# Filler matmuls in the waits of a kernel's boot, with one score buffer fewer (RWKV-6 attention and a dense pair, fp32)

## The chip, the core and the metric

The kernel runs on one core of one Trainium2 chip. The metric is the device time of one execution in microseconds (us). A core has a matrix engine (TensorE, PE in the profile, its weight loads PEld), a vector engine (VectorE, DVE), a scalar engine (ScalarE, ACT), GpSimd (POOL) and SyncE (SP), which here only issues transfers. [...]

## The reference, cut to what matters

```python
# attention: r, k, v, w of (4, 8, 768, 48), u of (8, 48)
for t in range(S):
    cur = np.einsum('bhd,bhe->bhde', u[None] * kt, vt)
    y[:, :, t] = np.einsum('bhd,bhde->bhe', rt, state + cur)
    state = wt[:, :, :, None] * state + np.einsum('bhd,bhe->bhde', kt, vt)
# x: y as (3072, 384); w_in (384, 2048), w_out (2048, 384)
h = x @ w_in
g = h - np.tanh(h)
return g @ w_out
```

Each head carries a 48x48 state through 768 time steps, with a decay w per step. The result, with the heads beside each other, goes through two dense layers. All of it is fp32.

## The kernel before, in words

The work is cut into eight blocks: four batches by two halves of the sequence (384 steps each). A block has an attention part and a dense part. The dense part of block i runs while the attention part of block i+1 is laid between its matmuls, by a plan written out by hand (`plan`, L531). For the first block there is no dense part to hide behind: its attention is done by `boot` (L565) at the start of the kernel. The order of instructions on TensorE, VectorE, ScalarE and SyncE is that of the program.

The attention of a block works on 64-step chunks. Heads lie in pairs, two heads of 48 in one tile of 128 partitions; the four pairs form two halves, h1 (pairs 2 and 3) and h2 (pairs 0 and 1). The scores of a chunk are built by levels. Level 1 takes products of neighbouring steps, with u, from the tiles `rmix` and `kmix` (made by ScalarE and VectorE in `mix`, L220 and L222). Levels 2, 4, 8, 16 and 32 multiply blocks of ever greater size. For each, `gram` (L242) does 24 small matmuls per half from `kq` and `rp`; `decay` (L274, VectorE) then multiplies `kq` and `rp` in place by the decays, so it must wait until TensorE has read them, and the next level of that half must wait for the decay; VectorE writes the scores from PSUM under a mask (L249 and L302), or at level 16 ScalarE copies them (L295). `totals` (L260) multiplies the decays of neighbouring blocks. At level 32 (`last_level`, L319) the copies by ScalarE (L330) are put off until after `turn`.

Then `turn` transposes `kq` on TensorE (L342) and ScalarE copies it to `ks` (L344); `update` multiplies it by v (L360), and VectorE carries the state over the chunks, twelve dependent steps for each half (L371). The result of a half is the sum of two sets of 24 matmuls in one pair of PSUM tiles: scores by v (`from_scores`, L406) and states by r (`from_states`, L388); between the sets TensorE drains and waits for it (`fence`, L418 and L424). In the boot, h1 takes the scores first and then the states, h2 the states first. ScalarE copies the result to `late` and `xT` (L434), a few small transfers fill holes in `xT`, and the first dense matmul (L484) can begin. A later block's inputs and the dense weights are loaded during the boot too; some of these transfers begin behind a given instruction (`begin_behind`).

All PSUM tiles of the attention come from `scratch` (L178): a tile of two banks in a pool. In the boot the pool has four such tiles[...]. A tile can be used again when what reads it is done. After the boot the pool is replaced by others.

The dense part takes 16 slices of 128 hidden columns: three matmuls for h (L484), an activation made of ScalarE and VectorE operations (L491 to L509), and three matmuls for the output (L522) three slices later.

Of the kernel before, what the change touches and what calls it, by code (L numbers as in the profile page):

```python
# [37 lines left out]
F32 = mybir.dt.float32  # L38
# [6 lines left out]
PSUM = bass.MemoryType.PSUM  # L45
# [3 lines left out]
P = 128  # L49
L = 64  # L50
NB = 384
# [33 lines left out]
def kernel(  # L85
# [10 lines left out]
    nc = tc.nc  # L96

    const = ctx.enter_context(tc.tile_pool(name="const", bufs=1))
# [13 lines left out]
    u_sb = const.tile([P, NPAIR], F32, name="u_sb", tag="u_sb")  # L112
    nc.scalar.dma_start(out=u_sb, in_=uT)

    warm = const.tile([P, 1], F32, name="warm", tag="warm")
    nc.scalar.activation(out=warm, in_=shift[:, 0:1], func=AF.Copy)

# [47 lines left out]
    def convert(f, raw, _):  # L165

        lo, hi = raw[:, :, 0], raw[:, :, 1]
        a = w_sb[:, f, :].bitcast(I32)
        up = conv.tile([P, 2 * DM], I32, name="up", tag="up", bufs=3)
        nc.scalar.activation(out=a.bitcast(F32), in_=hi.bitcast(F32), func=AF.Prelu,  # L170
                             scale=HIGH_SCALE, alpha=NEGATIVE)
        nc.scalar.activation(out=up, in_=lo.bitcast(U32), func=AF.Copy, scale=2.0 ** -29)
        return [
            lambda: nc.vector.tensor_single_scalar(a, a, 3, op=ALU.logical_shift_left),
            lambda: nc.vector.tensor_tensor(out=a, in0=a, in1=up, op=ALU.add)]  # L175
# [372 lines left out]
    blocks = [Block(b, q) for b in range(B) for q in range(NQ)]  # L548
# [3 lines left out]
    def more_weights(queue):  # L552
        raws.append(load_weights(more_weights.n, queue))
        more_weights.n += 1
        return raws[-1][-1]
# [3 lines left out]
    def begin_behind(ins, dma):  # L559


        tc.add_manual_dep(dma.ins, ins.ins.name, mybir.DependencyInfo(
            mybir.DependencyClass.Sync, mybir.DependencyReason.DATA))

    def boot(ps, blk, later):  # L565

        h1, h2 = HALVES
        for p0 in HALVES:
            for name, src in (("kq", kT), ("rp", rT), ("wt", wT)):
                blk.load(name, src, p0, UP)  # L570
        for name in ("rmix", "kmix"):
            blk.tiles[name] = inp.tile([P, NPAIR * NB], F32, name=name, tag=name)
        more_weights(nc.sync)
        blk.load_v()
        for _ in range(2):
            more_weights(nc.sync)
        blk.mix(h1, UP, copy=nc.vector.tensor_copy)
        masked = blk.level_1(ps, h1)
        blk.decay(1, h1, UP)
        blk.totals(1, h1, UP)  # L580
        blk.mix(h2, UP, copy=nc.scalar.copy)
        masked()
        blk.level(ps, 2, h1, UP)
        masked = blk.level_1(ps, h2)
        blk.decay(1, h2, UP)
        blk.totals(1, h2, UP)
        for m in (2, 4, 8, 16):
            blk.totals(m, h1, UP)
        masked()
        background = {2: lambda: later.load("rmix", rT, 0, NPAIR), 8: lambda: later.load("kmix", kT, 0, NPAIR),  # L590
                      16: lambda: later.load("wt", wT, 0, NPAIR), 32: lambda: more_weights(nc.sync)}
        ready, last = [], []
        for m in (2, 4, 8, 16, 32):
            for p0 in HALVES:
                if (m, p0) != (2, h1):
                    ins = blk.level(ps, m, p0, UP, last)
                if p0 == h2 or m == 32:
                    blk.totals(m, p0, UP)
            if m in background:
                begin_behind(ins, background[m]())  # L600
            if m <= 8:
                ready.append(convert(*raws.pop(0)))
            if m == 8:
                later.mix(0, NPAIR, ("rmix",))

        def converted():
            for op in ready.pop(0):
                op()

        more_weights(nc.sync)  # L610
        for p0 in HALVES:
            blk.turn(ps, p0)
        for copies in last:
            copies()
        later.mix(0, NPAIR, ("kmix",))
        for p0 in HALVES:
            blk.update(ps, p0)

        blk.result_2(*blk.result_1(ps, [h1, h1 + 1], "from_scores"), True, "from_states")
        blk.fill_holes([nc.sync, nc.scalar, nc.gpsimd])  # L620
        converted()
        ready.append(convert(*raws.pop(0)))
        converted()
        ins = blk.result_2(*blk.result_1(ps, [h2, h2 + 1]), True)
        begin_behind(ins, more_weights(nc.sync))
        later.load("kq", kT, 0, NPAIR)
        later.load("rp", rT, 0, NPAIR)
        while ready:
            converted()
        for name in ("totals 1", "totals 2"):  # L630
            later.prepare(name)
        for name in ("kq", "rp"):
            ready.append(convert(*raws.pop(0)))
            converted()
            later.prepare(name)

    with tc.tile_pool(name="ps_boot", bufs=4, space=PSUM) as ps_boot:
        xT = blocks[0].begin()
        boot(ps_boot, blocks[0], blocks[1])
    ps_d = ctx.enter_context(tc.tile_pool(name="ps_d", bufs=1, space=PSUM))  # L640
    ps_a = ctx.enter_context(tc.tile_pool(name="ps_a", bufs=2, space=PSUM))
    waiting, rest, extra = [], [], []
# [11 lines left out]
    for i, blk in enumerate(blocks):  # L654
        here = xT
        later = blocks[i + 1] if i + 1 < len(blocks) else None
# [5 lines left out]
        for f in range(NF):  # L662
# [15 lines left out]
            name, ins = loads.get(f), None  # L678
# [67 lines left out]
```

## Time and profile before

| | us |
|---|---|
| median of 4 runs (666.69 to 668.73) | 667.31 |
| profiled execution | 665.43 |
| its span, first to last instruction | 663.3 |
| TensorE busy | 641.4 |
| VectorE busy | 545.1 |
| ScalarE busy | 489.8 |
| first dense matmul (L484) starts at | 42.73 |
| first output matmul (L522) starts at | 56.99 |

All times inside a profile count from the start of the span. One fp32 matmul of the program stands in the profile as two MATMUL records and two LDWEIGHTS records; a transpose as one of each. "Idle before" is the time in which the engine stood before an instruction, with what ended it; "issue" means that the profile shows nothing that it waited for. PEclk is the share of TensorE's clock that was granted. The q8 queue of the transfers carries instructions.

### The profile page before, as it was taken

The numbers are of one execution on the slowest core, as the hardware profiler recorded it, in microseconds if no ns is written. First come the engines' busy times: TensorE is split into PE (matmuls) and PEld (weight loads), VectorE is DVE, ScalarE is ACT, GpSimd is POOL, SyncE is SP. The second block draws the span as 40 slices with busy tenths as digits, with TensorE's granted clock in tenths as the row PEclk, the third lists the DMA queues.
The fourth block names the chain that finished last, engine by engine and source line by source line (L and its number), as shares of the span: only waits on it lengthen the run. The fifth ranks groups of instructions, "written<-read, shape, count | busy, mean of one in ns | idle before, by whom it ended". The sixth has DMA issues, their size and how long they took to land.

```text
span 663.3 us, 19968 instructions
## 1 busy us (share of the span) xinstructions
PE 641.4 (97%) x8480; PEld 408.8 (62%) x8480; DVE 545.1 (82%) x1101; ACT 489.8 (74%) x968; POOL 4.8 (1%) x19
## 2 busy tenths in 40 slices
PE   5869999999999999999999999999999999999997
PEld 4745556566665666666666666656666566665554
DVE  7789999899768997599886997689975899757764
ACT  4779999876768667785767758686677857778785
POOL 2000000000000000000000000000000000000000
PEclk9969999999999999999999999999999999999999
DMA  8756433431303122221212231123131200000001
GB/s 319 232 180 224 132 130 121 142 121 50 97 11 115 54 67 80 58 72 53 94 50 57 74 97 52 50 64 112 49 97 29 101 3 2 1 12 37 0 0 37
DMA packets 30841, 54.37 MB, mean 82 GB/s; under 512 B 2336, under 2 KB 28704, under 8 KB 30752
## 3 DMA queue, kind: packets, MB, share of 16 engines
q1 hardware_dynamic: 30336, 52.80, 24.8%
q8 instruction: 67, 1.10, 0.7%
q10 hardware_dynamic: 352, 0.25, 0.1%
q14 instruction: 22, 0.18, 0.1%
q0 software_dynamic: 64, 0.05, 0.0%
HBM read 47.19 MB, written 4.72 MB: 78 GB/s over the span
## 4 chain that ended last, share of the span: by engine, by line
PE 86%; DVE 7%; ACT 2%; DMA 2%; issue 2%; PEld 0%; SPq 0%; PEldq 0%; DVEq 0%
PE acc L522 36%; PE hp L484 34%; PE att L242 8%; PE att L406 2%; PE att L388 2%; PE att L342 2%; PE att L360 1%; DVE hs L501 1%; DVE rp L274 1%; PE att L319 1%; DMA kq<-in_kT 1%; DVE kq L274 1%; DVE scores L302 1%; DVE w_sb L175 1%; DMA wt<-in_wT 1%
## 5 line engine op out<-in xcount | busy, mean ns | idle before, releaser
L484 PE MATMUL hp<-xT,w_sb 128*128 128x384 f32 x768 | 272.3, 491 | 4.1 <-ACT xT L434 2.1
L522 PE MATMUL acc<-w_sb,gT 128*128 128x384 f32 x768 | 273.7, 493 | 0.8
L484 PEld LDWEIGHTS hp<-xT,w_sb 128*128 128x128 f32 x768 | 145.2, 191 | 107.2 <-ACT xT L434 2.3
L522 PEld LDWEIGHTS acc<-w_sb,gT 128*128 128x128 f32 x768 | 140.5, 190 | 89.9 <-ACT o L527 2.3
L491 ACT ACTIVATE h<-hp 128x384 f32<-128x384 f32 x128 | 62.6, 489 | 125.5 <-PE hp L484 124.7
L506 DVE TENSOR_TENSOR th<-h,th 128x384 f32<-128x384 f32 x128 | 71.1, 555 | 45.7 <-ACT th L495 45.7
L501 DVE SCALAR_TENSOR_TENSOR hs<-h,s 128x384 f32<-128x384 f32 x128 | 71.1, 556 | 25.0 <-ACT s L492 25.0
L509 DVE COPY_PREDICATED gT<-big,th 128x384 f32<-128x384 int32 x128 | 76.3, 596 | 12.4
L493 ACT ACTIVATE qa<-s,shift 128x384 f32<-128x384 f32 x128 | 78.8, 615 | 4.2
L501 DVE SCALAR_TENSOR_TENSOR gT<-qb,hs 128x384 f32<-128x384 f32 x128 | 71.4, 558 | 9.3
L496 ACT ACTIVATE big<-s,shift 128x384 f32<-128x384 f32 x128 | 76.8, 600 | 0.0
L494 ACT ACTIVATE qb<-s,shift 128x384 f32<-128x384 f32 x128 | 76.7, 600 | 0.0
L501 DVE SCALAR_TENSOR_TENSOR hs<-qa,hs 128x384 f32<-128x384 f32 x128 | 70.7, 552 | 0.0
L492 ACT ACTIVATE s<-h 128x384 f32<-128x384 f32 x128 | 67.0, 524 | 4.0
L495 ACT ACTIVATE th<-h 128x384 f32<-128x384 f32 x128 | 64.9, 507 | 0.0
L242 PEld LDWEIGHTS att<-rp,kq 48*64 48x64 f32 x3072 | 53.3, 145 | 18.1 <-issue 11.7
L242 PE MATMUL att<-rp,kq 48*64 48x32 f32 x3072 | 57.2, 229 | 1.9 <-DVE rp L274 1.1
L274 DVE TENSOR_TENSOR kq<-kq,tot 128x768 f32<-128x768 f32 (+1 forms) x45 | 38.7, 860 | 2.3 <-PE att L319 1.4
L274 DVE TENSOR_TENSOR rp<-rp,tot 128x768 f32<-128x768 f32 (+1 forms) x45 | 38.9, 865 | 0.0
L371 DVE SCALAR_TENSOR_TENSOR states<-states,tot,att 128x48 f32<-128x48 f32 x176 | 31.5, 260 | 8.9 <-PE att L360 8.9
L302 DVE COPY_PREDICATED scores<-mask_all,att 128x384 f32<-128x384 uint8 (+1 forms) x54 | 31.9, 658 | 0.0
L242 PE MATMUL att<-rmix,kmix 48*64 48x64 f32 x768 | 14.6, 233 | 7.2 <-ACT rmix L222 7.2
(54 smaller groups left out, 335.6 us busy)
## 6 DMA issues: line engine op xcount, KB each, us to landing
raw<-in_weights SPq DMA_DIRECT2D x16, 768.0 KB, 4.4
rmix<-in_rT SPq DMA_DIRECT2D x7, 768.0 KB, 4.8
kmix<-in_kT SPq DMA_DIRECT2D x7, 768.0 KB, 4.6
wt<-in_wT SPq DMA_DIRECT2D x7, 768.0 KB, 4.6
kq<-in_kT SPq DMA_DIRECT2D x7, 768.0 KB, 5.6
rp<-in_rT SPq DMA_DIRECT2D x7, 768.0 KB, 4.6
v_sb<-in_v SPq DMA_DIRECT2D x8, 576.0 KB, 4.0
out_y<-o SPq DMA_DIRECT2D x23, 192.0 KB, 1.9
```

Source lines behind the costliest of these rows:

```text
L242: nc.tensor.matmul(dst, lhsT=lhs[rows, t0:t0 + L], rhs=src, start=True, stop=True)
L274: ins = nc.vector.tensor_tensor(out=part, in0=part, in1=by, op=ALU.mult)
L484: nc.tensor.matmul(hp, lhsT=w_in_sb[:, f, kc, :], rhs=xT[:, kc, :], start=(kc == KC - 1), stop=(kc == 0))
L492: nc.scalar.activation(out=s, in_=h, func=AF.Square)
L493: nc.scalar.activation(out=qa, in_=s, func=AF.Square, bias=shift[:, 0:1])
L494: nc.scalar.activation(out=qb, in_=s, func=AF.Square, bias=shift[:, 1:2])
L495: nc.scalar.activation(out=th, in_=h, func=AF.Tanh)
L496: nc.scalar.activation(out=big, in_=s, func=AF.Relu, bias=shift[:, 2:3])
L501: return lambda: nc.vector.scalar_tensor_tensor(out=out, in0=in0, scalar=scalar, in1=in1, op0=op0, op1=ALU.mult)
L506: lambda: nc.vector.tensor_tensor(out=th, in0=h, in1=th, op=ALU.subtract),
L509: lambda: nc.vector.copy_predicated(out=g, mask=big.bitcast(I32), data=th)], made
L522: nc.tensor.matmul(acc, lhsT=g[:, j * P:(j + 1) * P], rhs=w_out_sb[:, f, :], start=(f == 0), stop=(f == NF - 1))
```

## The change

A constant tile of ones is written by VectorE at the start. A new pool holds one PSUM tile `spare` of one bank, and the boot's pool for scores has three tiles and not four. In the boot, `keep_busy(n)` does n matmuls of 128x128 by 128x384 in fp32 from the constant tile into `spare`, which nobody reads: four ahead of everything, and one after each group of score matmuls (level 1 and level 2 of h1, level 1 of h2, and then each level of each half): sixteen in all. Nothing else is changed. In the changed kernel the lines after L114 stand two to fifteen lines further down (L242 is L244, L319 is L321, L342 is L344, L360 is L362, L388 is L390, L406 is L408, L484 is L486); the filler is L575.

```diff
+    idle_in = const.tile([P, NB], F32, name="idle_in", tag="idle_in")
+    nc.vector.memset(idle_in, 1.0)
...
-    def boot(ps, blk, later):
+    def boot(ps, ps_idle, blk, later):
 
         h1, h2 = HALVES
+        spare = ps_idle.tile([P, NB], F32, name="spare", tag="spare")
+
+        def keep_busy(n):
+
+            for _ in range(n):
+                nc.tensor.matmul(spare, lhsT=idle_in[:, 0:P], rhs=idle_in, start=True, stop=True)
+
+        keep_busy(4)
...
         masked = blk.level_1(ps, h1)
+        keep_busy(1)
         blk.decay(1, h1, UP)
...
         blk.level(ps, 2, h1, UP)
+        keep_busy(1)
         masked = blk.level_1(ps, h2)
+        keep_busy(1)
         blk.decay(1, h2, UP)
...
                 if (m, p0) != (2, h1):
                     ins = blk.level(ps, m, p0, UP, last)
+                    keep_busy(1)
...
-    with tc.tile_pool(name="ps_boot", bufs=4, space=PSUM) as ps_boot:
+    with tc.tile_pool(name="ps_boot", bufs=3, space=PSUM) as ps_boot, \
+            tc.tile_pool(name="ps_idle", bufs=1, space=PSUM) as ps_idle:
         xT = blocks[0].begin()
-        boot(ps_boot, blocks[0], blocks[1])
+        boot(ps_boot, ps_idle, blocks[0], blocks[1])
```

## The prediction

> **What bounds the kernel now.** I read the page, then busy time by stretch, then groups by shape, then the time line of TensorE in the boot (0 to 42.7 us, when the first dense matmul starts). The page:
>
> ```profile
> PE 641.4 (97%) x8480; PEld 408.8 (62%) x8480; DVE 545.1 (82%) x1101; ACT 489.8 (74%) x968; POOL 4.8 (1%) x19
> PEclk9969999999999999999999999999999999999999
> ```
>
> TensorE is the bound, except in the boot, and nothing after it has slack: what the boot gains or loses reaches the end. Stretches of 5 us show the only recorded loss of clock (PEclk is the third figure from the end):
>
> ```profile
> 35.00:40.00 5.00, 3.72 (x131) 3.25 (x135) 4.57 (x7) 3.40 (x6) 1.30 (x2) 0.69 0.13 34
> 40.00:45.00 5.00, 2.93 (x32) 1.81 (x24) 4.44 (x9) 3.80 (x7) 0.00 (x0) 0.50 0.54 173
> ```
>
> The half clock lasts from 36.85 to 47.09 us. Before 30 us the record says full, but the durations don't: the same shapes, first in the boot, then later.
>
> ```profile
> L242 PE MATMUL att<-rp,kq 48*64 48x32 f32 x379 | 12.0, 292 | 1.6 <-DVE rp L274 1.1 <-issue 0.4
> ...
> L342 PE MATMUL att<-ident,kq 128*128 128x128 f32 x12 | 2.8, 422 | 0.0
> ...
> L242 PE MATMUL att<-rp,kq 48*64 48x32 f32 x2304 | 38.4, 220 | 0.0
> ...
> L342 PE MATMUL att<-ident,kq 128*128 128x128 f32 x72 | 8.8, 273 | 0.0
> ```
>
> So TensorE is cold up to 30 us (in L360 the step between matmuls falls there from 27 to 15 ns). The time line (start, length, what, count, idle before and its releaser):
>
> ```profile
> 6.29 1.56 PE L242 MATMUL att<-rmix,kmix 48*64 48x64 f32 x48 [6.29 <-ACT rmix L222]
> 7.97 1.51 PE L242 MATMUL att<-rp,kq 48*64 48x32 f32 x48
> 10.36 1.56 PE L242 MATMUL att<-rmix,kmix 48*64 48x64 f32 x48 [0.89 <-ACT rmix L222]
> 12.45 2.35 PE L242 MATMUL att<-rp,kq 48*64 48x32 f32 x78 [0.53 <-DVE rp L274]
> 15.24 2.13 PE L242 MATMUL att<-rp,kq 48*64 48x32 f32 x66 [0.44 <-issue]
> 17.90 6.03 PE L242 MATMUL att<-rp,kq 48*64 48x32 f32 x187 [0.53 <-DVE rp L274]
> 24.09 0.43 PE L242 MATMUL att<-rp,kq 48*64 48x32 f32 x5 [0.16 <-issue]
> 24.45 0.76 PE L319 MATMUL att<-rp,kq 48*32 48x32 f32 x48
> 25.74 0.74 PE L319 MATMUL att<-rp,kq 48*32 48x32 f32 x48 [0.54 <-DVE tot L260]
> 26.41 2.82 PE L342 MATMUL att<-ident,kq 128*128 128x128 f32 x12
> 29.16 1.99 PE L360 MATMUL att<-v_sb,ks 64*64 64x48 f32 x96
> 31.29 0.55 PE L406 MATMUL att<-scores,v_sb 64*48 64x64 f32 x24
> 32.58 0.54 PE L406 MATMUL att<-scores,v_sb 64*48 64x64 f32 x21 [0.74 <-ACT scores L330]
> 35.10 0.31 PE L406 MATMUL att<-scores,v_sb 64*48 64x64 f32 x3 [1.98 <-issue]
> 35.50 0.99 PE L388 MATMUL att<-rp,states 48*48 48x64 f32 x52
> ```
>
> Two readings. From 9.6 to 24 us VectorE is never idle (4.90 and 5.00 of 5 us at 10 and at 15): its 1.45 to 1.6 us per half of a level pace the levels, and it waits for TensorE once, 0.66 us at 24.56. And TensorE stops three times in the middle of a group, for nothing but "issue": after 222 matmuls, 253 more (66+187) and 254 more (5+48+48+12+96+24+21). With a load each and some semaphore instructions that is 512 instructions each time. The instruction queue moves one packet ahead of each:
>
> ```profile
> q8 instruction: 1, 0.02, 5.9%
> ```
>
> (This is 32.8 to 33.8 us; others start at 12.86, 16.81, 21.83, 26.35 and 36.64.) A stop ends 1.28 to 1.38 us after a packet is in. [...]
>
> [...]
>
> **The change, part by part.** An fp32 matmul of 128x384 is two records, 0.64 us apart cold and 0.32 warm (43.53 to 46.09 and 48.94 to 50.23 us at L484).
>
> The memset on VectorE, 0.38 us (as L146), is hidden in its 1.01 us wait for the first kq; without that cover it would cost 0.4.
>
> Four matmuls ahead: 8 x 0.64 = 5.1 us from about 1.75, after the memset, so to 6.6 (clock rises on the way) or 7.0, where the first scores start at 6.29. Those end warm (0.8 us for 48, as 38.4/2304 x 48) by 7.9, and the mask, for which VectorE gets free at 8.30, doesn't notice. Cover gone, at most 0.7.
>
> I take it that these 5 dense us raise the clock by 6 to 8 us: 2.7 us of transposes and 0.9 of L360 did at 30.03. The bounds are no rise at all (second rival) and a rise at once, which VectorE's own pace would turn into nothing here.
>
> Twelve single ones: warm 0.65 plus 0.2 for changing shape; with a group's 0.8 that is 1.65 us per half, no better than VectorE's 1.45 to 1.6. So the warm clock buys nothing in the levels that the fillers don't spend, and at most the 0.66 us at 24.56.
>
> They also add 64 instructions, so block edges fall on earlier work: on matmul 12 of level 4 first half, 40 of level 8 first, 16 of level 16 second, 44 of level 32 second, and 12 of the first L406 group. Edge times: about 14.9, 19.25 (14.9+4.35), 23.65 (+4.4), 28.25 (+4.6, as 24.09 to 26.35+1.01+1.35). The first three cost VectorE nothing. But level 32's second half would stand at its edge at 26.8 and **must wait till 28.25**; it ended at 26.4 before. Then a filler (0.84), and the transposes start at 29.2 instead of 26.41. Warm, six take 0.73 (8.8/72 each) and not 1.28, so the copy ks 1 starts at 30.1 instead of 27.99.
>
> Three buffers. Up to level 32 the buffer is free before the data (each gram needs a decay that is later than the read of the buffer three back). Afterwards the put-off copies of level 32 hold two, so in the built program both turns and the first update share one: turn 2 waits for the copy ks 1 and update 1 for ks 2, with the other update and L406 queued behind on TensorE and VectorE's states waiting for them. ks 1 30.1 to 30.9, turn 2 31.0 to 31.9, ks 2 to 32.7, update 1 to 33.6: states start at 33.7 instead of 30.53. ScalarE's put-off copies (L330, 2.56) follow ks 2, to 35.25. The second L406 half waits for twelve state steps (2.15): 35.85. With 0.34 and the drain L388 starts at 36.5 against 35.50. **The lost 3.2 us shrink to 1.0**, because the 1.98 us stop disappears: its edge now lies 16 matmuls before[...].
>
> Then late copies (two, 0.97) to 38.4 release L388's second half; but its edge ([...]+3.8 as 35.10 to 36.64+0.92+1.35) allows 39.1 against 37.47. Warm, it takes 1.0 and L406 1.0: ScalarE's xT copies start at 41.1 against 40.74, +0.4. Cold it is +1.5. Since the idle between 31.8 and 35.1 is now partly filled, I expect the fall in the middle: **+1.0 us**. The dense L484 at half clock stay: no filler lies after level 32. If they were warm too, 2 us less of them would bring at most 0.5, as ScalarE reaches h only at 47.17 behind a weight's transfer.
>
> Against the profiled execution, 665.43 (span 663.3 and 2.1 around), this gives 666.4; the median shown, 667.31, is 1.9 above it, so 668.3.
>
> **Rivals.** First, faster: the edge at level 32 doesn't bind[...]. Then the transposes start at 27.4, everything after is 1.75 earlier, the late edge takes back 0.3: L406 ends 1.5 earlier than before, 665.8. For it: the middle stop at 24.09 is short, 0.16; against: three stops with one period. Second, slower: the clock isn't raised by the first four[...]. Then each filler takes 1.45 and each half of a level 2.7 on TensorE, which becomes the bound of the levels: from 15.4, after the first three groups, the nine further halves (the last two of 2.1) end near 37 instead of 26.4, some 10 us later and 677; it decides from level 2 on, and half of it if the clock rises midway. Against it: 5 us dense. Third, nothing: fetch and chain cancel exactly, 667.3.
>
> **How the numbers follow.** A measurement of this kernel can tell about 0.2%, 1.33 us. My forecast 0.60 (its own range 667.3 to 669.8: 0.36 within, 0.24 slower, when the last L388 and L406 are cold[...]); edge not binding 0.18 (0.15 faster, 0.03 within); cold 0.14, slower; nothing 0.08, within. Sum: faster 0.15, same 0.47, slower 0.38. Range 665.6 to 671.0: first, third and forecast, and the mild part of cold.
>
> **What would show it.** L242 at about 220 ns from 8 us on (else the second rival); an "issue" wait inside L321 (the shifted L319) near 27 to 28 us, none inside L408; transposes in two pieces with a ks copy between; states after 33 us; the xT copies 0.4 to 1.5 later. I am wrong if TensorE passes level 32 before 27.5, or if the clock stays full through 47 us and first dense work moves earlier by over 1 us.

## The result and the profile after

| | before | after |
|---|---|---|
| median, us (runs) | 667.38 (54) | 669.76 (35) |
| lowest to highest, us | 665.37 to 669.90 | 668.03 to 679.09 |
| profiled execution, us | 665.43 | 670.24 |
| span, us | 663.3 | 668.5 |
| ScalarE's last xT copies start at, us | 40.74 | 46.03 |
| first dense matmul starts at, us | 42.73 | 48.02 |

The ratio after to before is 1.0044 (95% interval 1.0034 to 1.0054), which is 2.9 us of 667.38 (it compares means); the medians differ by 2.4. The changed kernel is slower.

The two profiled executions differ by 4.8 us, about twice as much. The profile of the kernel before is one of its quicker runs: of 63 that stood beside the first experiments, those with a recorded mean clock of 0.992, as in the profile, took 666.24 us on average (19 runs), and those with 0.990 took 668.2 (32 runs). The profile of the changed kernel, with 0.990, is 0.5 above its median. So the traces show the places, and the medians give the size.

TensorE's row of the page, and its clock:

```profile
PE 650.2 (97%) x8512; PEld 408.6 (61%) x8512; DVE 546.2 (82%) x1102; ACT 490.0 (73%) x968; POOL 4.6 (1%) x19
PEclk9969999999999999999999999999999999999999
```

TensorE has 8.8 us more work, and the share of the span that it is busy is the same 97%. The row says nothing of the cause. The groups by shape of the first 24 us (busy us, mean ns, idle before) do:

```profile
L575 PE MATMUL spare<-idle_in 128*128 128x384 f32 x26 | 13.7, 638 | 1.5 <-DVE idle_in L116 1.5
L244 PE MATMUL att<-rp,kq 48*64 48x32 f32 x336 | 6.8, 221 | 1.6 <-issue 1.6
```

The same score matmuls took 292 ns before and take 221 now: the clock is up in the levels. What that saves, the fillers spend. The stretches of 5 us show where the clock is lost (third figure from the end):

```profile
35.00:40.00 5.00, 2.66 (x100) 2.17 (x102) 4.85 (x26) 2.70 (x8) 0.00 (x0) 0.80 0.26 104
40.00:45.00 5.00, 4.00 (x119) 3.51 (x123) 4.00 (x6) 3.31 (x6) 1.11 (x2) 0.50 0.15 34
45.00:50.00 5.00, 2.93 (x39) 1.91 (x32) 4.29 (x10) 3.87 (x7) 0.00 (x0) 0.50 0.50 162
```

The half clock lasts from 38.05 to 51.7 us, 13.65 us, where it lasted 10.24 in the profile before. The time line of TensorE (start, length, what, count, idle before and its releaser):

```profile
1.49 5.49 PE L575 MATMUL spare<-idle_in 128*128 128x384 f32 x8 [1.49 <-DVE idle_in L116]
6.90 1.10 PE L244 MATMUL att<-rmix,kmix 48*64 48x64 f32 x48
...
15.10 0.77 PE L244 MATMUL att<-rp,kq 48*64 48x32 f32 x35 [0.30 <-issue]
...
19.87 0.32 PE L244 MATMUL att<-rp,kq 48*64 48x32 f32 x8 [0.77 <-issue]
...
24.31 0.90 PE L244 MATMUL att<-rp,kq 48*64 48x32 f32 x48
25.14 0.91 PE L575 MATMUL spare<-idle_in 128*128 128x384 f32 x2
25.98 0.62 PE L321 MATMUL att<-rp,kq 48*32 48x32 f32 x48
26.54 0.91 PE L575 MATMUL spare<-idle_in 128*128 128x384 f32 x2
27.38 0.59 PE L321 MATMUL att<-rp,kq 48*32 48x32 f32 x44
29.39 0.25 PE L321 MATMUL att<-rp,kq 48*32 48x32 f32 x4 [1.43 <-issue]
29.57 0.91 PE L575 MATMUL spare<-idle_in 128*128 128x384 f32 x2
30.32 0.82 PE L344 MATMUL att<-ident,kq 128*128 128x128 f32 x6
32.03 0.88 PE L344 MATMUL att<-ident,kq 128*128 128x128 f32 x6 [0.89 <-ACT ks L346]
33.79 0.92 PE L362 MATMUL att<-v_sb,ks 64*64 64x48 f32 x48 [0.89 <-ACT ks L346]
34.96 0.92 PE L362 MATMUL att<-v_sb,ks 64*64 64x48 f32 x48 [0.25 <-ACT scores L332]
36.25 0.43 PE L408 MATMUL att<-scores,v_sb 64*48 64x64 f32 x12 [0.38 <-ACT scores L332]
38.53 1.30 PE L408 MATMUL att<-scores,v_sb 64*48 64x64 f32 x36 [1.85 <-issue]
39.95 1.73 PE L390 MATMUL att<-rp,states 48*48 48x64 f32 x52
42.56 1.74 PE L390 MATMUL att<-rp,states 48*64 48x64 f32 x44 [0.88 <-ACT late L436]
```

Four things are to be seen. The stops for "issue" in the middle of a group stand where the count of instructions put them: after matmul 12 or 13 of one level 4 group, 40 of a level 8 group, 44 of level 32's second half, and 12 of the first L408 group. In both traces they lie 256 TensorE instructions apart (matmuls, loads and semaphore instructions), or twice that: 512 from the stop that ends at 15.24 to that at 24.09 and 512 more to 35.10 in the kernel before; 256, 512 and 256 from 15.10 by 19.87 and 29.39 to 38.53 here. I call each such 256th instruction an edge, and those between two edges a block. Level 32 stands 1.43 us. The transposes (L344) come in two pieces with a ks copy between them, and VectorE's states begin only at 34.77 (30.53 before). And in L408 there is still a stop of 1.85 us, to 38.53. L390 starts 4.45 us later than L388 did before (35.50). The states, before and after:

```profile
30.53 4.29 DVE L371 SCALAR_TENSOR_TENSOR states<-states,tot,att 128x48 f32<-128x48 f32 x24 [2.81 <-PE att L360]
```

```profile
34.77 4.29 DVE L373 SCALAR_TENSOR_TENSOR states<-states,tot,att 128x48 f32<-128x48 f32 x24 [3.98 <-PE att L362]
```

They are 24 steps, twelve for each half, so the first half's twelve take 2.15 us.

The last instruction packet ahead of the end of this stop moved from 36.32 to 37.28 us, behind the two raw weight transfers that were issued at 30.75, and TensorE went on 1.25 us after it:

```profile
30.75 0.81 SPq L164 DMA_DIRECT2D raw<-in_weights  x2
```

```profile
q8 instruction: 1, 0.02, 5.0%
```

### The profile page after: what moved, and what is told of

Same layout as the page of the kernel before. It is cut to its first block, busy times and chain, and to the rows that moved or that the text cites. A ratio compares the mean times of both kernels' runs of the same rounds, so it can differ in the third digit from the quotient of the medians.

```text
span 668.5 us, 20035 instructions
## 1 busy us (share of the span) xinstructions
PE 650.2 (97%) x8512; PEld 408.6 (61%) x8512; DVE 546.2 (82%) x1102; ACT 490.0 (73%) x968; POOL 4.6 (1%) x19
## 3 DMA queue, kind: packets, MB, share of 16 engines
HBM read 47.19 MB, written 4.72 MB: 78 GB/s over the span
## 4 chain that ended last, share of the span: by engine, by line
PE 91%; ACT 3%; DVE 3%; issue 2%; PEld 0%; PEldq 0%; DVEq 0%
PE hp L486 36%; PE acc L524 36%; PE att L244 9%; PE spare L575 2%; PE att L390 2%; PE att L408 2%; PE att L344 1%; PE att L362 1%; PE att L321 1%; DVE w_sb L177 1%; ACT scores L332 1%; DVE hs L503 1%; ACT h L493 0%; DVE gT L511 0%; ACT xT L436 0%
## 5 line engine op out<-in xcount | busy, mean ns | idle before, releaser
L486 PE MATMUL hp<-xT,w_sb 128*128 128x384 f32 x768 | 272.1, 491 | 4.3 <-ACT xT L436 2.1
L486 PEld LDWEIGHTS hp<-xT,w_sb 128*128 128x128 f32 x768 | 145.2, 191 | 107.5 <-ACT big L498 2.5
L244 PEld LDWEIGHTS att<-rp,kq 48*64 48x64 f32 x3072 | 48.4, 135 | 21.5 <-issue 17.0
L244 PE MATMUL att<-rp,kq 48*64 48x32 f32 x3072 | 52.5, 220 | 1.6 <-issue 1.6
L172 ACT ACTIVATE w_sb<-raw 128x768 f32<-128x768 f32 x16 | 14.6, 911 | 4.9 <-DMA raw<-in_weights 4.7
```

The costliest lines, as they stand in the source:

```text
L244: nc.tensor.matmul(dst, lhsT=lhs[rows, t0:t0 + L], rhs=src, start=True, stop=True)
L486: nc.tensor.matmul(hp, lhsT=w_in_sb[:, f, kc, :], rhs=xT[:, kc, :], start=(kc == KC - 1), stop=(kc == 0))
```

## The experiments

**My theory after the result.** From L390 on, everything waits for the later of two chains: VectorE's states, and the block of instructions that L408 runs into. In the kernel before, the block came at 35.10 and the first half's states were done at 32.7 (30.53 and 2.15), so there were 2.4 us of cover for the states. The third buffer and the fillers' shifted block edge each take some of it; both together take more than there is. **Rivals:** the single fillers' own time is the cost; the lost buffer alone is the cost; the weights that block the instruction packet are the cost.

### One part alone: three buffers

```diff
-    with tc.tile_pool(name="ps_boot", bufs=4, space=PSUM) as ps_boot:
+    with tc.tile_pool(name="ps_boot", bufs=3, space=PSUM) as ps_boot:
```

> The kernel before with three score buffers and no fillers. Theory A (the third buffer's chain at the turn and the fetch of instructions make the loss): the transposes come in two pieces with a ks copy between, the states start near 32.4 us instead of 30.5[...]: 1.5 to 2.5 us slower than before (ratio 1.002 to 1.004). Rival B (the fillers' own time on TensorE and the clock make the loss): within 0.5 us of before.

Measured: 667.87 us (14 runs), ratio 1.0001 (0.9986 to 1.0015). Here the transposes stood in two pieces too, from 26.77 and 29.19 us, and the states began at 33.22, 2.7 later than before, without a cost in the median that can be measured (the interval leaves room for 1 us). So the lost buffer alone doesn't make the 2.4 us. The profile can't say more: it is of the longest of the 14 runs, 669.86, in which L388 started at 37.92 after a stop of 0.94 us.

### The fourth buffer given back after the levels

The changed kernel, but the fillers' bank is closed after the last filler, and a pool of one score tile takes its place for the second transpose and the second update.

```diff
-        for p0 in HALVES:
-            blk.turn(ps, p0)
+        for p0, pool in zip(HALVES, (ps, ps_more)):
+            blk.turn(pool, p0)
...
-        for p0 in HALVES:
-            blk.update(ps, p0)
+        for p0, pool in zip(HALVES, (ps, ps_more)):
+            blk.update(pool, p0)
```

> The changed kernel with the fourth score buffer given back after the last filler (the fillers' pool is closed and a pool of one score tile opened for the second turn and update). Theory A: turn 2 no longer waits for ks 1 and update 1 only for ks 1, the states start about 2.5 us earlier than in the changed kernel, near 32.3 us; [...]so 2 to 3 us are gained back: ratio to before 1.000 to 1.001. Rival B: as the changed kernel, 1.004.

Measured: 665.66 us (22 runs, one of them 675.23), ratio 0.9978 (0.9963 to 0.9992). All sixteen fillers are there, and the kernel is faster than before. Its time line of TensorE:

```profile
26.59 0.59 PE L321 MATMUL att<-rp,kq 48*32 48x32 f32 x44
28.77 0.25 PE L321 MATMUL att<-rp,kq 48*32 48x32 f32 x4 [1.59 <-issue]
...
29.70 1.47 PE L344 MATMUL att<-ident,kq 128*128 128x128 f32 x12
31.41 1.62 PE L362 MATMUL att<-v_sb,ks 64*64 64x48 f32 x96 [0.23 <-ACT ks L346]
...
34.51 0.76 PE L408 MATMUL att<-scores,v_sb 64*48 64x64 f32 x36 [0.81 <-issue]
35.38 0.99 PE L390 MATMUL att<-rp,states 48*48 48x64 f32 x52
```

The stop in level 32 is as long as in the changed kernel, and the transposes stand in one piece. L390 starts at 35.38, as before the change (35.50), and not at 39.95. The next block of instructions also came earlier: the stop in L408 ends at 34.51 and not at 38.53; the second transposes no longer wait for the first ks copy. The states began at 32.39 here, 1.9 later than before, and the cover held.

### Smaller fillers

```diff
+            cols = NB if n == 4 else 32
             for _ in range(n):
-                nc.tensor.matmul(spare, lhsT=idle_in[:, 0:P], rhs=idle_in, start=True, stop=True)
+                nc.tensor.matmul(spare[:, 0:cols], lhsT=idle_in[:, 0:P], rhs=idle_in[:, 0:cols],
+                                 start=True, stop=True)
```

> The changed kernel with the twelve single fillers cut to 32 columns, so with as many instructions but a fraction of their time; the four ahead stay whole. Theory A (instruction blocks and buffers): the stops stay at the same matmuls (12 of level 4, 40 of level 8, 44 of level 32, 12 of the first L406 group) and the turn stays in two pieces; level 32 is through some 1 us earlier (28.3), the time is 0 to 1.5 us better than the changed kernel: ratio to before 1.002 to 1.0045. Rival B (the fillers' time): all of the loss goes, ratio 1.000 or below. Open: whether the clock holds with small matmuls alone.

Measured: 669.79 us (22 runs), ratio 1.0038 (1.0025 to 1.005), the same as the changed kernel. The number of instructions is the same. The single fillers are shorter, but the clock falls: the L244 group at 7.92 us takes 0.90 us and those from 11.84 on 1.51, so that a half of a level again takes 2.0 us and not 1.67. The states begin at 35.94, L390 at 39.28. Here the two chains end together: L408 stands only 0.30 us for its block, to 37.87, and the first half's states are done at 38.09. What the large fillers cost they pay back through the clock: their own time isn't the loss, but neither does this run show them as free.

> The small single fillers (32 columns) with the fourth score buffer given back for the turn. If the singles' dense time gains or loses nothing, as with three buffers: 0.997 to 0.999, as with whole fillers and the fourth buffer. If the warm clock that whole singles hold through the turn is worth something: 0.999 to 1.001, with L362 and L408 at about 300 ns.

The small fillers with the fourth buffer given back: 666.02 us (22 runs), ratio 0.9973 (0.9962 to 0.9984). With either size of filler, the buffer is worth about 0.65%. In this profile the clock was down in most of the levels and at the turn (L244 takes 1.51 us for 48 at 15.33 us and 23.52, the twelve transposes 2.80; with whole fillers 0.90 and 1.47), so the clock that the whole fillers hold up there is worth nothing that can be measured (0.9978 with them).

### Four fillers ahead and no others

```diff
+    idle_in = const.tile([P, NB], F32, name="idle_in", tag="idle_in")
+    nc.vector.memset(idle_in, 1.0)
...
+        spare = scratch(ps)[:, 0, 0:NB]
+        for _ in range(4):
+            nc.tensor.matmul(spare, lhsT=idle_in[:, 0:P], rhs=idle_in, start=True, stop=True)
```

> The kernel before with its four score buffers and only the four fillers ahead, written into a score tile that is given back at once. If the clock that they raise holds through the levels, L244 takes about 220 ns, the 0.66 us wait of VectorE at level 16 goes and the transposes are warm: the states start 1 to 1.5 us earlier; but block edges still pace TensorE, and the stop in L406 stands against the same weights. Theory A: 0 to 1 us faster than before (ratio 0.9985 to 1.000). Rival B (the clock falls again in the levels, small matmuls don't hold it): 1.000 with L244 near 290 ns from about 14 us on.

Measured, with four buffers: 665.59 us (18 runs), ratio 0.997 (0.9958 to 0.9982). That is faster than either expectation, although the clock fell at 10.3 us (0.53 granted from 10 to 15 us, 0.50 from 15 to 30), as rival B had it.

> The four fillers ahead alone, with three score buffers: with the changed kernel (1.004), the fourth buffer given back (0.998) and the four ahead alone with four buffers (0.997) it fills the square of single fillers and buffers. If the third buffer costs by itself once the clock is raised early: 1.002 to 1.004. If it costs only together with the single fillers (whose 48 instructions put the block edge into level 32, ahead of the turn[...]): 0.997 to 0.999,[...] the stop in L408 no longer than 2.3 us.

Measured, with three: 666.21 us (22 runs), ratio 0.9972 (0.996 to 0.9984). So three buffers cost nothing that can be measured here either; with intervals of 0.0012 to each side, some 1 us could hide. The time lines, first with four buffers, then with three:

```profile
31.95 0.43 PE L408 MATMUL att<-scores,v_sb 64*48 64x64 f32 x12 [0.47 <-ACT scores L332]
34.63 0.67 PE L408 MATMUL att<-scores,v_sb 64*48 64x64 f32 x12 [2.25 <-issue]
35.38 1.73 PE L390 MATMUL att<-rp,states 48*48 48x64 f32 x52
```

```profile
34.16 0.86 PE L408 MATMUL att<-scores,v_sb 64*48 64x64 f32 x24
35.50 1.13 PE L408 MATMUL att<-scores,v_sb 64*48 64x64 f32 x24 [0.48 <-DVE states L373]
36.72 1.73 PE L390 MATMUL att<-rp,states 48*48 48x64 f32 x52
```

With four buffers L408 stands for its instructions. With three, the wait for the states has taken the place of that stop, and L390 starts 1.34 us later in these profiles. The wait is new: with four buffers, L408's second half waits for ScalarE's copies alone (0.47 us), and only L390 takes the states, step by step. With three it waits for all twelve steps (0.49, 0.48 and 0.48 us in three profiles with three buffers). L408 reads no states, so what it waits for must be a tile of PSUM that the steps still read.

Put together, ratios to the runs of the kernel before that stood beside each (their medians were 667.4, 667.6 and 668.0). In the two lower rows three buffers serve the levels in both columns, and the columns differ from the transposes on:

| fillers | four buffers from the transposes on | three |
|---|---|---|
| none | 1 | 1.0001 |
| four ahead | 0.997 | 0.9972 |
| four ahead, twelve single | 0.9978 | **1.0044** |
| four ahead, twelve small single | 0.9973 | **1.0038** |

**The loss is in neither part: it is their meeting.** On top of four ahead, the third buffer changes the ratio by 0.0002, the singles by 0.0008, and both by 0.0074. The profiles of these four kernels say where. They are one execution each, and the half clock falls differently in each, so only the large steps count:

| | states start | first half's done (+2.15) | L408 goes on at | L390 |
|---|---|---|---|---|
| four ahead | 30.12 | 32.27 | 34.63, its block | 35.38 |
| with singles | 32.39 | 34.54 | 34.51, its block | 35.38 |
| with three buffers | 33.16 | 35.31 | 35.50, states | 36.72 |
| with both (the change) | 34.77 | 36.92 | 38.53, its block | 39.95 |

With four buffers the singles move L390 by nothing: the 2.27 us by which they delay the states fit into the 2.36 between 32.27 and 34.63. With three buffers the same singles move it by 3.23 in these profiles: about half because the states, which have no cover left, let go 1.61 later (36.92 for 35.31), and about half because the block comes 1.61 later still (38.53 for 36.92). That the meeting costs is shown by the ratios; this split is read from single executions.

### The weights that stand ahead of the instruction packet

```diff
-                      16: lambda: later.load("wt", wT, 0, NPAIR), 32: lambda: more_weights(nc.sync)}
+                      16: lambda: later.load("wt", wT, 0, NPAIR)}
...
-        more_weights(nc.sync)
         for p0 in HALVES:
             blk.turn(ps, p0)
...
         for p0 in HALVES:
-            blk.update(ps, p0)
+            ins = blk.update(ps, p0)
+            if p0 == h1:
+                begin_behind(ins, more_weights(nc.sync))
+                more_weights(nc.sync)
```

> The changed kernel with the two weight transfers that began behind the last decay of level 32 now behind the twelve state steps of h1. Theory A[...]: the packet moves within 1 to 2 us of the first update, near 35 us instead of 36.3, the stop of 1.85 us in L408 goes or shrinks below 0.5, 1 to 2 us come back: ratio to before 1.001 to 1.003. Rival B (the clock and the third buffer alone make the loss, the block would be late anyway): 1.004, and the stop stays at 1.5 us or more.

Measured, in the changed kernel: 670.72 us (5 runs), ratio 1.0062 (1.0045 to 1.0078), slower than either expectation. The stretches of 1 us (last figure: GB/s) and the time line:

```profile
30.00:31.00 1.00, 0.38 (x2) 0.00 (x0) 0.00 (x0) 0.58 (x1) 0.00 (x0) 0.50 0.00 0
31.00:32.00 1.00, 0.73 (x4) 0.73 (x5) 0.00 (x0) 0.22 (x1) 0.00 (x0) 0.50 0.00 0
32.00:33.00 1.00, 0.81 (x4) 0.41 (x2) 0.00 (x0) 0.15 (x1) 0.00 (x0) 0.50 0.06 16
```

```profile
28.04 0.25 PE L321 MATMUL att<-rp,kq 48*32 48x32 f32 x4 [1.42 <-issue]
...
31.27 1.54 PE L344 MATMUL att<-ident,kq 128*128 128x128 f32 x6 [0.89 <-ACT ks L346]
...
37.63 0.89 PE L408 MATMUL att<-scores,v_sb 64*48 64x64 f32 x24 [0.48 <-DVE states L373]
38.63 1.73 PE L390 MATMUL att<-rp,states 48*48 48x64 f32 x52
```

This tells two things. First, the transfers stood idle from 30 to 32 us, TensorE had passed the edge at 28.04, and yet the packet moved only at 32.43, 1.2 us after the second transposes began. **The packet doesn't follow the edge at a fixed time:** it moved 4.4 us after it here, and 0.65 after the edge at 39.80 in the kernel before (40.45). Here TensorE was held by the ks copy until 31.27, and the packet moved only behind that; what sets it off, no trace shows. Second, the stop of 1.85 us in L408 is gone, so the weights did hold up the packet. What it was worth stays unsettled. By the ratio nothing is won back; but in this profile, of the quickest of the five runs (669.31), the last xT copies start at 44.66, 1.4 us earlier than in the changed kernel's, although L408's second half now waits for the states, which began at 35.30 as the clock was down from 29.05 on (0.53 granted from 29 to 30 us, 0.50 from 30 to 40).

> The same move of the two weight transfers in the kernel before. Theory A: its stop of 1.98 us in the second L406 half shrinks by 1 us or more (block usable near 33.5 instead of 35.1), L388 starts near 34: 0.5 to 1.5 us faster than before, ratio 0.998 to 0.999. Rival B: the transfers then come too late for ScalarE's conversion at 38.5 us, and what is won is lost there: 1.000 to 1.001.

The same in the kernel before: 666.05 us (4 runs), ratio 1.0 (0.9982 to 1.0017).

```profile
33.36 0.99 PE L388 MATMUL att<-rp,states 48*48 48x64 f32 x52
...
36.37 0.66 PE L406 MATMUL att<-scores,v_sb 64*48 64x64 f32 x27
39.71 0.88 PE L406 MATMUL att<-scores,v_sb 64*48 64x64 f32 x21 [2.68 <-issue]
```

L388 starts 2.1 us earlier than before, and the last L406 group then stands 2.68 us at the next edge: the xT copies start at 40.64 against 40.74. ScalarE waited there for TensorE (2.20 us) and not for weights, so the number is that of rival B, but the place isn't. The stop that was removed came back at the next edge.

> The kernel before with the four fillers ahead alone (four score buffers) and the two weight transfers later. Theory A: both gains add, the stop of 2.25 us in L408 shrinks by over 1 us: ratio to before 0.995 to 0.996. Rival B: as with the four ahead alone, 0.997.

Both moves together, four ahead and the weights later: 664.69 us (6 runs), ratio 0.9979 (0.9962 to 0.9996), which can't be told from four ahead alone. L390 started at 32.67, and the last L408 group then stood 1.98 us at its edge. The first dense matmul started at 41.37, 1.4 us earlier than in the kernel before, and the span was only 0.4 shorter (662.9).

### No fillers ahead

```diff
-        keep_busy(4)
```

> The changed kernel without the four fillers ahead. If the twelve single ones raise the clock by themselves soon[...]: as the changed kernel, 1.003 to 1.006. If they don't, each half of a level takes 2.7 us on TensorE, L244 stays near 290 ns to 30 us and level 32 ends near 36 us: 1.012 to 1.018. Theory A expects the first[...].

Measured: six runs, 668.37, 668.74 and 668.84, and 677.95, 678.75 and 678.86. Two levels, so no mean describes them. The profiled one is of the second kind:

```profile
27.11 1.51 PE L244 MATMUL att<-rp,kq 48*64 48x32 f32 x48
28.55 1.65 PE L575 MATMUL spare<-idle_in 128*128 128x384 f32 x2
30.13 1.51 PE L244 MATMUL att<-rp,kq 48*64 48x32 f32 x48
...
38.42 0.76 PE L321 MATMUL att<-rp,kq 48*32 48x32 f32 x48
```

A half of a level takes 3.0 us, and level 32 is left at 39 us: this is the second rival of the prediction, with its 677 us (it had 2.7 us for a half). The transposes at 40.55 us are the first work that is quicker: 1.20 us for six, where six take 1.54 at half clock. As far as lengths tell, the four ahead keep this off in nearly all runs: one of the changed kernel's 35, 679.09, has such a length all the same, but there is no profile of that one.

### Fillers at the end of the boot

```diff
+        busy(1)
         blk.fill_holes([nc.sync, nc.scalar, nc.gpsimd])
...
+        busy(3)
         begin_behind(ins, more_weights(nc.sync))
```

> The kernel before with four fillers ahead, one after the first half's L390 and three after the last L408, in score tiles that are free then, to have the clock up again for the first dense matmuls. If the half clock there (36 to 47 us) costs: [...]0.5 to 1 us better than the four ahead alone: 0.995 to 0.9965. If ScalarE's h behind the weights sets the pace there anyway: 0.997, and if the fillers stand before L486 when xT is ready, 0.998.

Four ahead, then one filler after the first L390 group and three after the last L408: 666.52 us (22 runs), ratio 0.998 (0.9969 to 0.9992). The first dense matmuls are warm (2.17 us for six), but start at 45.20 and not at 43.27 as with four ahead alone: the last fillers end only at 45.09, while the xT copies are done at 43.84. What the warm start brings, the fillers take.

> The kernel before once more, for a second profile of it beside the first, whose 665.43 us lies at the lower end of its runs: the stops in the middle of groups come after the same 222, 253 and 254 matmuls[...].

A second profile of the kernel before: 665.70 us, recorded clock 0.992 again. The second and third stop stand on the same matmuls as in the first profile (23.87 and 35.16 us). The first, after 222, is missing: the group that holds that matmul runs through (2.81 us for 96 from 11.95). Both profiles lie below the kernel's median.

## Why the prediction was right, and where it was wrong

The 669.76 us lie inside the range, 665.6 to 671.0, and barely inside the forecast's own 667.3 to 669.8. The forecast said 1.0 us more, which the prediction itself held for too little to measure (0.47 for "same", 0.38 for "slower"); it was 2.4 by the medians. The range held partly by luck. From profile to profile the forecast was 3.8 us short (4.8 and not 1.0). Most of that is balanced by the step from a profile to a median, 1.9 up for the kernel before and 0.5 down for the changed one.

Of its signs, L244 at 220 ns, the wait inside level 32, the transposes in two pieces and the states after 33 us came. "None inside L408" did not (1.85 us), nor did xT copies only 0.4 to 1.5 us later (5.3).

**The memset and the four ahead: right.** The first scores start at 6.90 us (6.6 to 7.0 was said), the clock rises at 7.33 (6 to 8; the group at 6.90 takes 1.10 us, the next of its shape 0.93), and L244 takes 221 ns.

**Twelve single ones: right.** A half of a level takes 1.67 us on TensorE (1.65), of which a filler, to the start of the next group, takes 0.84 (25.14 to 25.98), as was said. Every stop stands on the matmul where an edge was put, within one. The reading that the stops come each 512 instructions was too narrow: in the changed kernel two of them lie 256 apart. The kernel before passed every other edge without a stop (19.68, 29.45 and 39.80 us).

**The edge at level 32: right in kind, 1.1 us short.** It was to let go at 28.25 and did at 29.39. The edge before it was put at 23.65, on the author's estimate of 4.4 us from one edge to the next (19.68 to 24.09 in the kernel before); TensorE itself got there only at 24.55, because the fillers' 1.67 us per half and the two earlier stops had by then put it behind. Nor is 4.4 us a fixed price: it is 4.84 here (24.55 to 29.39), and some 3.5 without any stop in the kernel before with its weights moved (an estimate: by count the edges lie in its L360 group, which starts at 29.27, and near the end of its L406 group, which starts at 32.70).

**Three buffers: right.** One transposed half waits for the other's copy, and the states start at 34.77; 33.7 was said, and the 1.07 between is the edge's 1.14.

**The failed step:** "because the 1.98 us stop disappears: its edge now lies 16 matmuls before". It didn't: L408 stood 1.85 us, to 38.53, where the states alone would have let go at 36.92. The step counted the block from the moment when TensorE passes the edge before it, 28.25 there, as if it came a fixed time later; that was the author's assumption, and the runs don't show it. In the changed kernel with its weights moved, the packet moved 1.2 us after the second transposes had begun, 4.4 us after the edge. Here these transposes waited for ks 1, for want of the fourth buffer, until 32.03, and by then the weights (30.75) stood ahead of the packet, which moved at 36.32, 6.93 us after the edge. The prediction counted the wait for ks 1 in the states' chain and left it out of the block's. This step is 1.6 us in the profile; what it is worth in the median isn't shown.

**The rest of the sum is mostly the clock.** L408's last 36 matmuls and the drain took 1.42 us (0.65 in the sum, for 24), and from L390's start to the xT copies it was 6.08 us, where the middle of the forecast had 5.24: 1.6 in all. At full clock such 36 took 0.87 (the fourth buffer given back, 34.51 to 35.38), and at half clock without a stop at an edge the second stretch took 5.90 (four ahead with three buffers, 36.72 to 42.62); so some 1.2 of the 1.6 is half clock, the rest the twelve more matmuls behind the stop and the next edge. Together the xT copies start at 46.03 and not at 41.74: 1.07 for the edge at level 32, 1.6 for the stop and 1.6 for this. That is the 4.3 us by which they are later than the forecast's +1.0. The execution was 3.8 longer than forecast, as 0.1 of it was won again later, and 1.7 us and not 2.1 lie outside the span.

**The rivals.** The first, that the edge at level 32 doesn't bind, is out: it bound in every kernel with the singles that was profiled with the clock up, for 1.4 to 1.6 us. The second, a clock that stays low, is real without the four ahead. The third, that all cancels, is out by the interval.

**What stays open:** why the kernel with four ahead is 2.0 us faster in the median. Some 0.4 of it lies outside the span: in every kernel that writes the tile of ones, the runs are 1.7 us longer than their span, in every other 2.1; why, no trace shows. Its profiled execution (665.71) is no faster than that of before (665.43), and its xT copies start later, at 41.27. Its runs lie between 664.3 and 667.6, while half of before's are about 668.2. The recorded 0.990 of those, against 0.992, would be some 2.7 us more at half clock than the profile's 10.24 (an estimate: 0.002 x 663 us / 0.5), but none of them has a trace. So it stays open too whether three buffers alone, level with before in the median, cost something that the spread of these runs hides.

## What to carry to other kernels

Where a stop covers a chain, count its cover once: two edits that each fit under it may not fit together, so add their delays on each chain and take the later chain. An added instruction that nobody waits for still moves the places where the engine stops for instructions, and an edge that moves into a critical group can cost more than the instruction's own time (1.43 us at level 32, where a filler takes 0.65); with cover left, as with the fourth buffer given back, it costs nothing that can be measured. And before a wait is put down as gone, look at what else stood ahead of its end: here the packet moved 4.4 us after the edge where the waiting engine was itself held, and 6.93 where the weights stood ahead of it too.

## What the runs showed of the hardware

- **In both traces TensorE's stops for instructions in the boot lie 256 instructions apart, or 512.** For the 17103 TensorE instructions of the kernel before its page shows 67 packets of the q8 queue, one for 255. TensorE didn't stop at every 256th: the kernel before passed those at 19.68, 29.45 and 39.80. Where it stopped in the middle of a group there, it went on 4.41 us or more after the edge before (19.68 to 24.09) and 1.25 to 1.51 us after a packet was in; with its weights moved, the kernel before passed two edges some 3.5 us apart without a stop. A stop taken away at one edge came back at the next: 2.68 us there, and 1.98 with the four ahead as well. The four stops took 4.35 us of the changed kernel's boot.
- **The packet came at no fixed time after the edge.** It moved 0.65 us after it where TensorE ran on (39.80 and 40.45, the kernel before), and 6.93 us after it behind the weights (29.39 and 36.32, the changed kernel). With no weights ahead of it, it moved 4.4 us after it where TensorE was held (28.04 and 32.43, the changed kernel with its weights moved): only once TensorE had gone on by a filler and six transposes and had begun the next six. This is read from these three profiles, and what sets the packet off they don't show.
- **Which work raised the clock here.** Busy wasn't enough. Without the four ahead TensorE had no idle time from 10 to 40 us, with a filler of 1.65 us in every 3.0, and in the profiled run the clock stayed at half (score matmuls 293 ns). In the kernel before, 187 records of score matmuls from 17.90 to 23.93 us without a gap didn't raise it. Eight dense records, 5.49 us, raised it at 7.33. With four ahead alone it fell again at 10.3, and the small score matmuls, busy for 4.72 and 4.56 of 5 us from 15 to 25, didn't bring it back (0.50 granted); the single fillers held it to 38.05. Where the clock was down at the turn, the twelve transposes in one piece, or they and the update behind them, brought it up in all seven such profiles: the update takes 1.87 to 2.62 us and the next 24 of the scores by v 0.51 to 0.55, where they take 2.81 and 0.86 at half clock. In two pieces with 0.89 us between, as three buffers have them, they did so in none of three (2.81 us for the update in each, and 3.91 to 4.21 for the first six dense matmuls, from 44.61 us or later). Without the four ahead, with a filler of 1.65 us right before them, the first piece was quicker at 40.55.

```profile
L244 PE MATMUL att<-rp,kq 48*64 48x32 f32 x336 | 10.7, 292 | 0.9 <-issue 0.6 <-DVE rp L276 0.3
```

This is four ahead alone, 11 to 24 us: the score matmuls are back at 292 ns.
